# Attention scores of a fused attention and mixture-of-experts kernel: q and k handed over transposed, three 64-row products per head instead of two 128-row ones

## The chip, the cores and the metric

The kernel runs on one core of a Trainium2 chip. The engines that matter here are TensorE (PE, its weight loads are listed as PEld), VectorE (DVE), ScalarE (ACT), GpSimd (POOL), and SyncE (SP), which issues the DMA transfers. The metric is the time of one execution on the device in microseconds (us). The inputs are arranged on the host before the launch, and that is outside the measured time.

## What is computed

Attention with a block-causal mask, then a routed expert layer, then a dense layer with an x·sigmoid(x) activation. The change concerns the attention scores alone.

```python
def _attn_ref(q, k, v):                      # B, H, S, D = 4, 8, 576, 64
    scores = np.matmul(q, k.transpose(0, 1, 3, 2)) / np.sqrt(D)
    mask = pos[:, None] // 64 >= pos[None, :] // 64
    scores = np.where(mask, scores, -1e9)
    attn = softmax(scores)
    return np.matmul(attn, v)
# x = attention output, one row of 512 per token (2304 tokens)
# moe:  expert = argmax of a cosine score over 8 experts; out = gate * relu(x @ w1[e]) @ w2[e]
# moe2: h = x @ w_in; out = (h * sigmoid(h)) @ w_out
```

## The kernel before

**Stages.** The program first does the attention and then, in one long stage, the two layers behind it. The attention works on 16 pairs of heads (4 batches, 4 pairs each; the two heads of a pair are called hh = 0 and 1 here). A loop over i overlaps five steps of different pairs: the loads and splits of pair i + 3, the transposes of pair i + 2 (`x_units`), scores and softmax of pair i + 1 (`s_units`), the transposes of the probabilities of pair i (`v_units`), the products with v of pair i - 1 (`o_units`), and the scaling and expert scores of pair i - 2 (`e_units`). Beside these the loop converts one piece of a weight per pair (`conv`, tiles `wbits` and `wcv`).

**Precision.** A product of two fp32 numbers is made of fp32r products: each operand is split into a high part (`hi`, the fp32r rounding) and a low part (`lo`, the rest), and hi·hi, hi·lo and lo·hi are summed in PSUM.

**Scores before.** q and k of a pair arrive with tokens in the partitions and 64 numbers along the row. `split` writes hi and lo beside each other, [64 hi, 64 lo] for q and [64 lo, 64 hi] for k, so that a row is 128 wide. `x_units` transposes such 128×128 blocks on PE (9 for k, 9 for q of each pair) into PSUM, and ACT or DVE copies them to `QT` and `KT`: partitions 0 to 63 of q are hi, 64 to 127 are lo, and k the other way round. One product of 128 rows of `QT` and `KT` thus gives hi·lo + lo·hi. The second product uses `QH` and `KH`: hi parts in partitions 0 to 63, copied there by a DMA from `QT` and `KT` (`again`, tiles `qh` and `kh`), and the mask in partitions 64 to 127. So a head needs two products per score tile.

**Score units.** For a pair there are these units in `s_units`: `full(0)` and `full(1)` (128 queries, 576 keys, one head each, two pieces of 288 columns), `both(3)`, `both(2)`, `both(1)` (both heads, 448, 320 and 192 keys, the last computed as 256 columns) and `tiny` (64 keys). Each takes a PSUM tile `s` of two banks from the pool `ps_s`, which has two of them; head 0 lies in the first bank and head 1 in the second, and for `full` both banks hold one head. DVE takes the row maxima (`mx<-s`), ACT the exponentials with their sums (`p<-s,mx`), and then the PSUM tile is free.

**Order.** The class `_Plan` records all operations and sets their order on each engine from estimated costs (`_cost`); where an operation may run on ACT or DVE (`copy`, `either`), it chooses the engine by the estimated loads. Each engine then executes its instructions in that order. Nearly all instructions carry the line of the place where the plan issues them, L189, so they are told apart by their tiles.

**Names in the rows below.** `xk`, `xq`: transposes of k and q. `k0s`, `q0s`: splits of the first 64 tokens. `ks`, `qs`: splits. `pt`: transposes of probabilities. `o`: products with v. `e`: scaling and expert scores. `h`: the first product of the stage behind the attention. A form 128*64 means a product whose output takes 64 columns of the array, and 64*128 one that uses 64 of its rows.

Of the kernel before, what the change touches and what calls it, by code (L numbers as in the profile page):

```python
# [19 lines left out]
P = 128  # L20
# [59 lines left out]
class _Plan:  # L80
# [187 lines left out]
    def _cost(self, engine, method, args, kw):  # L268
# [20 lines left out]
        if engine == "tensor":  # L289
# [7 lines left out]
            if args[2].dtype == F32R:  # L297
                return max(n + 32, 2 * free(args[1])) / 2.4
# [190 lines left out]
def _attention(first, ctx, late, tc, plan, q, k, v, emb, tau, x_dram, identr, lr_all, ss_all, conv=None):  # L489
# [12 lines left out]
    sp = pool("a_split", 2, first)  # L502
# [8 lines left out]
    qk = pool("a_qk", 2, ctx)  # L511
    hi_p = pool("a_hi", 1, ctx)
# [10 lines left out]
    def load(i, what):  # L523


        b, hp = pairs[i]
        src = {"q": q, "k": k, "v": v}[what]
        t = (vp if what == "v" else ld).tile([P, 8, D], F32, tag=what, name=f"{what}_{i}")
        body = src[b, 2 * hp:2 * hp + 2, 64:S, :]
        rows = t.rearrange("p (h j) d -> p h j d", h=2)  # L530
# [9 lines left out]
    heads = {}  # L540

    def head(b, src, what):

        if what != "v":
            heads[b, what] = t = ld.tile([P, NPAIR, D], F32, tag=what + "0",
                                         name=f"{what}0_{b}", bufs=1)
        for hh in range(2):
            r0 = 64 * hh
            nc.sync.dma_start(
                (v0[b % 2][:, :, r0:r0 + 64] if what == "v" else t)[r0:r0 + 64],  # L550
                src[b, :, 0:64, :].rearrange("(a h) p d -> p h a d", h=2)[:, hh])
# [14 lines left out]


    QH, KH = ([hi_p.tile([P, 2, w], F32R, name=f"{n}{m}") for m in range(2)]
              for n, w in (("qh", S + 64), ("kh", S)))

    def masks(m, eq, ek):
# [1200 lines left out]
```

## Time and profile before

| | |
|---|---|
| median of 3 runs | 944.27 us (942.07 to 944.77) |
| profiled execution | 942.74 us, its span 941.0 us |
| PE busy over the span | 895.1 us (95%) |
| DVE busy | 747.8 us (79%) |
| ACT busy | 591.2 us (63%) |
| POOL busy | 107.0 us (11%) |
| share of 16 DMA engines, transfers issued by SP | 25.1% |

A busy time is the union of an engine's instructions. On PE the end of a matmul is modelled and includes the way through the array, so that neighbours overlap; what a matmul takes of PE's time is read from the distance between the starts of neighbours. The busy share of an engine is not the same in all stages, so the stages are read one by one.

### The profile page before, as it was taken

The page shows a single profiled execution, that of the slowest core. Times are in us where ns is not written, and L with a number is a line of the kernel's source. Part 1 is how long each engine was busy: PE and PEld are TensorE (multiplying, and loading weights), DVE is VectorE, ACT ScalarE, POOL GpSimd, SP SyncE. Part 2 cuts the span into 40 slices and gives each one's busy share as a digit, 9 for nine tenths or more (in the row PEclk, how much of TensorE's full clock was granted, in tenths as well). Part 3 has the DMA queues.
Part 4 walks back from the last instruction along what each step waited for, and adds up shares of the span by engine and source line. Part 5 has one row for each costly group of instructions (what it writes and reads, how often), then busy time and mean ns, then how long its engine had stood idle before and what let it go on. Part 6 is the DMA issues. An engine that isn't in the chain of part 4 may idle for free.

```text
span 941.0 us, 14120 instructions
## 1 busy us (share of the span) xinstructions
PE 895.1 (95%) x4890; PEld 744.3 (79%) x4890; DVE 747.8 (79%) x1367; ACT 591.2 (63%) x1214; POOL 107.0 (11%) x166
## 2 busy tenths in 40 slices
PE   2999999999889998999999999999999999999996
PEld 2777677776556787888888888888899998898895
DVE  6788989987798987999978888888666666667663
ACT  4878888887656765888876566676434334334332
POOL 4010111112200001010311111121101001001001
PEclk9999999999999999999999999999999999999998
DMA  6446657536224234775100033131211002000000
GB/s 179 121 127 165 176 137 215 134 117 230 75 86 145 101 112 154 266 250 172 54 27 23 23 111 133 41 125 62 78 46 51 18 1 64 4 1 34 1 0 34
DMA packets 67051, 91.63 MB, mean 97 GB/s; under 512 B 28888, under 2 KB 45272, under 8 KB 66976
## 3 DMA queue, kind: packets, MB, share of 16 engines
q1 hardware_dynamic: 61536, 72.32, 25.1%
q0 software_dynamic: 5440, 18.36, 5.6%
q8 instruction: 40, 0.66, 0.3%
q14 instruction: 35, 0.29, 0.1%
HBM read 123.23 MB, written 13.11 MB: 145 GB/s over the span
## 4 chain that ended last, share of the span: by engine, by line
PE 59%; issue 0%; DVE 0%; ACT 0%; POOL 0%; POOLq 0%; ACTq 0%
PE o L189 20%; PE g L189 19%; PE y L189 9%; PE h L189 9%; PE ht L189 1%; PE yt L189 1%; PE xt L189 1%; POOL out_dram L1524 0%; POOLq L1767 0%; DVE sg L189 0%; DVE ht L189 0%; ACT sg L189 0%; DVE yt L189 0%; DVE xt L189 0%; ACT ys L189 0%
## 5 line engine op out<-in xcount | busy, mean ns | idle before, releaser
L189 PE MATMUL o<-w,g 128*128 128x512 f32 x864 | 229.9, 398 | 0.0
L189 PE MATMUL g<-yt,w 128*128 128x384 f32 x1152 | 227.3, 337 | 0.2 <-issue 0.2
L189 PEld LDWEIGHTS g<-yt,w 128*128 128x128 f32 x1152 | 203.3, 188 | 13.0 <-issue 0.5
L189 PEld LDWEIGHTS o<-w,g 128*128 128x128 f32 x864 | 161.2, 189 | 31.0 <-DVE g L189 0.7
L189 ACT ACTIVATE sg<-g 128x384 f32<-128x384 f32 x96 | 47.4, 493 | 142.6 <-PE g L189 142.1
L189 PE MATMUL y<-w2s,ht 128*128 128x512 f32 x450 | 128.6, 400 | 0.7 <-DVE w2s L189 0.7
L189 PE MATMUL h<-w1s,xt 128*128 128x512 f32 x450 | 110.4, 396 | 0.7 <-ACT xt L189 0.5
L189 DVE TENSOR_TENSOR w1s<-wraw,w1s 128x1024 fp32r<-128x1024 f32 x75 | 91.5, 1223 | 19.3 <-ACT w1s L189 18.6
L189 PEld LDWEIGHTS h<-w1s,xt 128*128 128x128 f32 x450 | 84.2, 188 | 21.1 <-issue 1.7
L189 DVE TENSOR_TENSOR w2s<-wraw,w2s 128x1024 fp32r<-128x1024 f32 x75 | 91.2, 1223 | 11.6 <-ACT w2s L189 9.8
L189 PEld LDWEIGHTS y<-w2s,ht 128*128 128x128 f32 x450 | 81.1, 188 | 13.7 <-DVE w2s L189 1.0
L189 ACT ACTIVATE p<-s,mx 128x576 f32<-128x576 f32 (+4 forms) x160 | 83.1, 532 | 8.5 <-DVE mx L189 7.5
L189 DVE TENSOR_REDUCE mx<-s 128x1 f32<-128x576 f32 (+2 forms) x96 | 67.6, 709 | 20.8 <-PE s L189 16.4
L189 ACT CAST w2s<-wraw 128x1024 fp32r<-128x1024 f32 x66 | 69.4, 1053 | 19.7 <-PE h L189 8.5
L189 DVE TENSOR_TENSOR w<-win,w 128x512 fp32r<-128x512 f32 x96 | 65.9, 689 | 16.7 <-ACT w L189 16.6
L189 ACT CAST g<-sg 128x384 fp32r<-128x384 f32 x96 | 49.3, 514 | 43.9 <-DVE sg L189 43.0
L189 ACT CAST w1s<-wraw 128x1024 fp32r<-128x1024 f32 x61 | 64.4, 1059 | 17.8 <-PE y L189 7.8
L189 PE MATMUL o<-pt,v 128*64 128x256 f32 (+5 forms) x320 | 68.8, 450 | 0.2 <-ACT pt L189 0.2
L189 DVE TENSOR_TENSOR w<-wout,w 128x512 fp32r<-128x512 f32 x96 | 65.6, 683 | 2.5 <-ACT w L189 2.3
L189 ACT CAST w<-win 128x512 fp32r<-128x512 f32 x86 | 53.3, 622 | 21.3 <-PE o L189 21.0
L189 PE MATMUL pt<-ident,p 128*128 128x128 f32 (+1 forms) x400 | 61.6, 275 | 0.9 <-DVE pt L189 0.6
L189 DVE CAST w<-wout 128x512 fp32r<-128x512 f32 x53 | 22.6, 427 | 47.8 <-PE g L189 47.7
(208 smaller groups left out, 1293.1 us busy)
## 6 DMA issues: line engine op xcount, KB each, us to landing
wraw<-in_moe_w_dram SPq DMA_DIRECT2D x76, 1024.0 KB
wbits<-in_moe_w_in_dram SPq DMA_DIRECT2D x16, 512.0 KB
wbits<-in_moe_w_out_dram SPq DMA_DIRECT2D x16, 512.0 KB
kh<-kt SPq DMA_DIRECT2D x15, 288.0 KB
k<-in_k_dram SPq DMA_DIRECT2D x16, 256.0 KB
q<-in_q_dram SPq DMA_DIRECT2D x16, 256.0 KB
v<-in_v_dram SPq DMA_DIRECT2D x32, 128.0 KB
x_rows<-xe POOLq DMA_DIRECT2D x4, 1024.0 KB, 7.0
```

What stands on the lines that cost most here:

```text
L189: alts = {e: (lambda eng, m=m, a=a, k=k: getattr(eng, m)(*a, **k), self._cost(e, m, a, k), self._shares(e, m, a, k)) for e, m, a, k in calls}
```

## The change

The host passes q and k of each pair already transposed (`_layout`): partitions 0 to 63 hold the 64 numbers of head 0, partitions 64 to 127 those of head 1, and the 576 tokens lie along the row. The parts of v are rearranged on the host too, so that a partition's row is one piece of memory. `x_units`, `QT`, `KT`, `QH`, `KH`, their masks and the DMA copies `again` are gone. `split` makes hi and lo of a [128, 576] tile, as [128, 2, 576], with q scaled by 0.125 on the way. `scores` issues for each head three products of 64 rows (hi·hi, hi·lo, lo·hi), head 0 in PE's rows 0 to 63 and head 1 in rows 64 to 127, in turn, and a product of 64 columns from `maskq` and `maskk`, two constants, that adds the mask where a tile has one. All calls of a unit are recorded as one operation (`together`), and a 64-row fp32r product is estimated at half its cost. `full` now does both heads at once and takes both PSUM tiles of `ps_s`; `both(1)` computes 192 columns instead of 256. The loop starts at i = -2 instead of -3.

```diff
+    def together(self, calls):
+        costs = [self._cost("tensor", "matmul", c[:3], {}) for c in calls]
+        def f(eng):
+            for out, a, b, kw in calls:
+                eng.matmul(out, a, b, **kw)
+        self.call({"tensor": (f, sum(costs))}, [self._box(x) for c in calls for x in c[1:3]],
+                  list(dict.fromkeys(self._box(c[0]) for c in calls)))
...
             if args[2].dtype == F32R:
-                return max(n + 32, 2 * free(args[1])) / 2.4
+                part = 0.5 if args[1].shape[0] == 64 else 1.0
+                return max(n + 32, 2 * free(args[1])) / 2.4 * part
...
-    sp = pool("a_split", 2, first)
...
-    qk = pool("a_qk", 2, ctx)
-    hi_p = pool("a_hi", 1, ctx)
+    sp = pool("a_split", 3, ctx)
     ps_s = pool("ps_s", 2, ctx, space=PSUM)
...
         if what == "v":
-            for hh in range(2):
-                nc.sync.dma_start(rows[:, hh], body[hh].rearrange("(j p) d -> p j d", p=P))
+            t = vp.tile([P, 8, D], F32, tag=what, name=f"{what}_{i}")
+            nc.sync.dma_start(t, v[b, hp, :, 0:8, :])
...
         else:
-            nc.sync.dma_start(rows, body.rearrange("h (p j) d -> p h j d", p=P))
-        if hp == 0:
-            head(b, src, what)
+            t = ld.tile([P, S], F32, tag=what, name=f"{what}_{i}")
+            nc.sync.dma_start(t, {"q": q, "k": k}[what][b, hp])
...
-    def split(n, what, key, t, **kw):
-        hi, lo = (0, 1) if what == "q" else (1, 0)
-        spl[key] = s = sp.tile([P, n, 2, D], F32R, **kw)
-        nc.vector.tensor_copy(s[:, :, hi, :], t)
-        nc.sub(s[:, :, lo, :], t, s[:, :, hi, :].bitcast(F32))
+    def split(i):
+        t = raw[i, "k"]
+        spl[i, "k"] = s = sp.tile([P, 2, S], F32R, tag="k", name=f"ks_{i}")
+        nc.copy(s[:, 0], t)
+        nc.sub(s[:, 1], t, s[:, 0].bitcast(F32))
+        t = raw[i, "q"]
+        spl[i, "q"] = s = sp.tile([P, 2, S], F32R, tag="q", name=f"qs_{i}")
+        nc.either(("scalar", "activation", (s[:, 0], t, AF.Copy), dict(scale=0.125)),
+                  ("vector", "tensor_scalar_mul", (s[:, 0], t, 0.125), {}))
+        nc.vector.scalar_tensor_tensor(s[:, 1], t, 0.125, s[:, 0].bitcast(F32), ALU.mult,
+                                       ALU.subtract)
...
-                for j in range(4):
-                    nc.tensor.transpose(ps[:, j * P:(j + 1) * P], s[:, 4 * hh + j], identr)
...
-            for z, qs, ks, q0 in ((0, QT[i], KT[i], 0), (1, QH[i % 2], KH[i % 2], 64 * odd)):
-                c = slice(q0 + qcols(j), q0 + qcols(j) + n)
-                for out, hh, c0, w in parts:
-                    nc.tensor.matmul(out, qs[:, hh, c], ks[:, hh, c0:c0 + w],
-                                     start=(z == 0), stop=(z == 1))
+            qs, ks = spl[i, "q"], spl[i, "k"]
+            c = slice(qcols(j), qcols(j) + P)
+            calls = []
+            for z, (m, n) in enumerate(((0, 0), (0, 1), (1, 0))):
+                for out, hh, c0, w, mask in parts:
+                    r = slice(64 * hh, 64 * hh + 64)
+                    calls.append((out, qs[r, m, c], ks[r, n, c0:c0 + w],
+                                  dict(start=(z == 0), stop=(z == 2))))
+                if z == 1:
+                    for out, hh, c0, w, mask in parts:
+                        r = slice(64 * hh, 64 * hh + 64)
+                        if mask is not None:
+                            calls.append((out[:, mask:mask + 64], maskq[r], maskk[r],
+                                          dict(start=False, stop=False)))
+            nc.together(calls)
...
-        def full(hh):
-            def f():
-                if hh == 0:
-                    alloc()
-                ps = ps_s.tile([P, 2, 512], F32, tag="s", name=f"s4{hh}_{i}")
-                scores(4, *[(ps[:, a, 0:288], hh, 288 * a, 288) for a in range(2)])
+        def full():
+            alloc()
+            ps = [ps_s.tile([P, 2, 512], F32, tag="s", name=f"s4{hh}_{i}") for hh in range(2)]
+            scores(4, *[(ps[hh][:, a, 0:288], hh, 288 * a, 288, (64, 224)[hh] if a == hh else None)
+                        for a in range(2) for hh in range(2)])
+            for hh in range(2):
...
-        return [(0.55, full(0)), (0.55, full(1)), (0.8, both(3)), (0.6, both(2)),
+        return [(1.1, full), (0.8, both(3)), (0.6, both(2)),
                 (0.5, both(1)), (0.45, tiny)]
```

**PE in the middle of the attention.** Before, from the second score unit of pair 6 on (`s41_6`, `s3_6`, `s2_6` are its units; the numbers behind a unit's name are its pair and a buffer):

```order
L189 MATMUL s41_6_435<-kt_6_386,qt_6_385 128x288 x2
L189 MATMUL s41_6_435<-kh0_137,qh0_135 128x288 x2
L189 MATMUL xk1_7_437<-ident_62,ks_7_378 128x128 x4
L189 MATMUL o_4_432<-pt_4_380,v_4_333 64x512 x2
L189 MATMUL s3_6_440<-kt_6_386,qt_6_385 128x448 x2
L189 MATMUL s3_6_440<-kh0_137,qh0_135 128x448 x2
L189 MATMUL pt2_5_438<-ident_62,p_5_382 128x128 x4
L189 MATMUL xk2_7_442<-ident_62,k0s_1_274 128x128
L189 MATMUL o_4_432<-pt_4_380,v_4_333 64x384 x2
L189 MATMUL xq0_7_445<-ident_62,qs_7_379 128x128 x4
L189 MATMUL s2_6_446<-kt_6_386,qt_6_385 128x320 x2
L189 MATMUL s2_6_446<-kh0_137,qh0_135 128x320 x2
```

Now, from the last score units of pair 5 on:

```order
L189 MATMUL o_4_353<-pt_4_315,v_4_273 64x512 x2
L237 MATMUL s1_5_327<-ks_5_274,qs_5_275 128x192 x4
L237 MATMUL s1_5_327<-maskk_128,maskq_127 128x64 x2
L237 MATMUL s1_5_327<-ks_5_274,qs_5_275 128x192 x2
L237 MATMUL s0_5_333<-ks_5_274,qs_5_275 128x64 x6
L189 MATMUL pt0_5_347<-ident_62,p_5_310 128x128 x4
L189 MATMUL pt1_5_355<-ident_62,p_5_310 128x128 x4
L189 MATMUL o_4_353<-pt_4_315,v_4_273 64x384 x2
L189 MATMUL pt2_5_358<-ident_62,p_5_310 128x128 x4
L189 MATMUL pt4_5_365<-ident_62,p_5_310 128x128 x4
L237 MATMUL s40_6_349<-ks_6_308,qs_6_309 128x288
L237 MATMUL s41_6_350<-ks_6_308,qs_6_309 128x288
```

The transposes `xk` and `xq` are gone, two score units often stand next to each other, and in the units of two heads (here `s40_6` and `s41_6`) the heads take turns product by product.

**ACT at the same place.** Before, from pair 6's second copy of k on (`qt`, `kt` are the copies out of PSUM, `p` the exponentials):

```order
L189 CAST kt_6_386<-xk1_6_392 128x512
L189 ACTIVATE p_5_382,rs_139<-s40_5_383,mx_5_4_0_384 128x576
L189 COPY pt_4_380<-pt2_4_395 128x512
L189 ACTIVATE p_5_382,rs_139<-s41_5_393,mx_5_4_1_394 128x576
L189 COPY pt_4_380<-pt3_4_399 128x512
L189 ACTIVATE p_5_382,rs_139<-s3_5_397,mx_5_3_0_398 128x448 x2
L189 ACTIVATE qt_6_385<-xq0_6_400 128x512
L189 ACTIVATE p_5_382,rs_139<-s2_5_401,mx_5_2_0_402 128x320 x2
L189 ACTIVATE qt_6_385<-xq1_6_405 128x512
```

Now, for the same pair 5:

```order
L189 CAST ks_7_342<-k_7_305 128x576
L189 COPY pt_4_315<-pt4_4_329 128x512
L189 ACTIVATE qs_7_343<-q_7_306 128x576
L189 COPY pt_4_315<-pt3_4_326 128x512
L189 ACTIVATE p_5_310,rs_129<-s40_5_311,mx_5_4_0_313 128x576
L189 ACTIVATE p_5_310,rs_129<-s41_5_312,mx_5_4_1_314 128x576
L189 COPY ot_3_330<-o_3_317 128x512
L189 COPY pt_4_315<-pt6_4_335 128x64
L189 COPY ot_3_330<-o0_3_336 128x64
L189 ACTIVATE p_5_310,rs_129<-s3_5_321,mx_5_3_0_322 128x448 x2
L189 ACTIVATE p_5_310,rs_129<-s2_5_324,mx_5_2_0_325 128x320 x2
```

The copies `kt` and `qt` no longer stand between the exponentials; the first operation of a split (`ks`, `qs`) may now run on ACT, two pairs ahead of its use.

**ACT at the start.** Now, from the first split on (`wbits`, `wcv` belong to the weight conversion, `en_s` to the expert embedding):

```order
L189 ACTIVATE qs_139<-q_126 128x576
L189 ACT_TABLE_LOAD
L189 ACTIVATE en_s<-en_s 8x1
L189 CAST ks_146<-k_136 128x576
L189 ACT_TABLE_LOAD
L189 ACTIVATE en_s<-en_s 8x1
L189 ACTIVATE qs_147<-q_137 128x576
L189 CAST ks_165<-k_143 128x576
L189 ACTIVATE p_148,rs<-s_0_149,mx_4_0_151 128x576
L189 ACTIVATE p_148,rs<-s_0_150,mx_4_1_152 128x576
L189 ACTIVATE wcv_218<-wbits_217 128x512
L189 ACTIVATE wbits_217<-wbits_217 128x512
```

Before, `wcv` and `wbits` stood ahead of the first exponentials of pair 0; now a split of pair 2's k (`ks_165<-k_143`) stands there, and `wcv` behind the first two.

## Rows read from the trace of the kernel before

**Rows 1.** Stages: length, busy us (instructions) by engine, granted clock, DMA share, GB/s.

```profile
31.00:216.00 185.00, 180.63 (x1303) 139.51 (x1301) 165.14 (x401) 154.87 (x464) 19.81 (x18) 1.00 0.55 153
...
246.00:941.00 695.00, 671.16 (x3315) 572.36 (x3313) 544.14 (x860) 401.70 (x664) 69.81 (x85) 0.99 0.23 77
```

**Rows 2.** The page's chain of work that ended last: shares by engine.

```profile
PE 59%; issue 0%; DVE 0%; ACT 0%; POOL 0%; POOLq 0%; ACTq 0%
```

**Rows 3.** PE in time: start us, us, operation, form, count [idle before, releaser].

```profile
8.52 1.25 PE L189 MATMUL xk<-ident,ks 128*128 128x128 f32 x8 [8.52 <-DVE ks L189]
...
15.56 0.85 PE L189 MATMUL s<-kt,qt 128*128 128x288 f32 x2 [0.18 <-ACT qt L189]
...
23.79 1.12 PE L189 MATMUL s<-kt,qt 128*128 128x448 f32 x2 [4.78 <-ACT p L189]
...
31.30 0.53 PE L189 MATMUL s<-kt,qt 128*128 128x288 f32 x2 [0.15 <-ACT p L189]
...
216.04 0.53 PE L189 MATMUL s<-kt,qt 128*128 128x288 f32 x2 [0.69 <-ACT p L189]
...
245.75 3.60 PE L189 MATMUL h<-wraw,x 128*128 128x512 f32 x8
```

**Rows 4.** PE in time within one pair, from 104.8 to 114.6 us.

```profile
104.81 0.39 PE L189 MATMUL s<-kh,qh 128*128 128x64 f32 x2
105.03 1.09 PE L189 MATMUL pt<-ident,p 128*128 128x128 f32 x8
...
108.27 0.42 PE L189 MATMUL s<-kh,qh 128*128 128x288 f32 x2
108.62 0.27 PE L189 MATMUL pt<-ident,p 64*128 64x64 f32 x1
...
109.19 1.12 PE L189 MATMUL o<-pt,v 128*128 128x512 f32 x2
110.15 0.60 PE L189 MATMUL pt<-ident,p 128*128 128x128 f32 x4
110.51 0.54 PE L189 MATMUL xk<-ident,ks 128*128 128x128 f32 x4
110.89 0.50 PE L189 MATMUL s<-kt,qt 128*128 128x288 f32 x2
111.23 0.43 PE L189 MATMUL s<-kh,qh 128*128 128x288 f32 x2
111.50 0.60 PE L189 MATMUL pt<-ident,p 128*128 128x128 f32 x4
112.02 1.08 PE L189 MATMUL o<-pt,v 128*64 128x512 f32 x4
113.03 0.28 PE L189 MATMUL xk<-ident,k0s 128*128 128x128 f32 x1
113.15 0.63 PE L189 MATMUL s<-kt,qt 128*128 128x448 f32 x2
113.62 0.57 PE L189 MATMUL s<-kh,qh 128*128 128x448 f32 x2
114.03 0.60 PE L189 MATMUL pt<-ident,p 128*128 128x128 f32 x4
```

**Rows 5.** Attention by groups: operation, forms, count | busy us, mean ns | idle before.

```profile
L189 DVE TENSOR_TENSOR ks<-k,ks 128x512 fp32r<-128x512 f32 x16 | 12.7, 796 | 0.0
...
L189 ACT ACTIVATE qt<-xq 128x512 fp32r<-128x512 f32 x32 | 19.1, 602 | 4.5 <-PE xq L189 4.5
...
L189 ACT CAST kt<-xk 128x512 fp32r<-128x512 f32 x24 | 14.1, 588 | 3.3 <-PE xk L189 2.9
...
L189 ACT ACTIVATE wcv<-wbits 128x512 f32<-128x512 f32 x12 | 8.1, 677 | 4.4 <-DMA wbits<-in_moe_w_in_dram 4.4
```

**Rows 6.** The same groups for the softmax of one unit, `both(3)`.

```profile
L189 DVE TENSOR_REDUCE mx<-s 128x2 f32<-128x896 f32 x16 | 17.4, 1087 | 8.1 <-PE s L189 6.4 <-ACT qt L189 1.5 <-ACT wcv L189 0.2
...
L189 ACT ACTIVATE p<-s,mx 128x448 f32<-128x448 f32 x32 | 20.0, 633 | 1.0 <-DVE mx L189 0.8
```

More of the change, by code (lines that the diff above doesn't have):

```diff
@@ L538, in load @@
         raw[i, what] = t
[L540 to L551, printed above, removed]
-    spl = {}
@@ L583, in _attention @@
-    masks(0, nc.vector, nc.gpsimd)
-    plan.shift = 60
-    masks(1, nc.gpsimd, nc.gpsimd)
-    plan.shift = 0
+    maskq = cp.tile([P, P], F32R, name="maskq")
+    maskk = cp.tile([P, 64], F32R, name="maskk")
+    nc.vector.memset(maskq.bitcast(F32), 0.0)
+    nc.gpsimd.memset(maskk.bitcast(F32), 0.0)
+    for r0 in (0, 64):
+        nc.vector.memset(maskq.bitcast(F32)[r0:r0 + 1, 0:64], NEG)
+        nc.gpsimd.memset(maskk.bitcast(F32)[r0:r0 + 1], 1.0)
     rs = cp.tile([P, B, 5, H], F32, name="rs")
@@ L702, in _attention @@
+    PR, PT, OT, XE, LG = {}, {}, {}, {}, {}
     WID = {j: 2 * P * j + P for j in (4, 3, 2, 1)}
@@ L771, in tiny @@
             rows = slice(r0, r0 + 64)
-            out = slice(0, r0 + 64)
-            scores(0, (ps[out, 0, 0:64], 0, 512, 64), (ps[out, 1, 0:64], 1, 0, 64))
+            scores(0, (ps[:, 0, 0:64], 0, 512, 64, None), (ps[:, 1, 0:64], 1, 0, 64, None))
             c0 = PO[0]
@@ L944, in inter @@
         return _merge([(1.0, f) for _, f in a], [(1.0, f) for _, f in c])
-    for i in range(-3, NP + 2):
-        if i == -3:
+    for i in range(-2, NP + 2):
+        if i == -2:
             esq = experts()
@@ L950, in _attention @@
             expert_rows(esq)
-        if 0 < i + 4 < NP:
+        if 0 < i + 3 < NP:
             for w in "kq":
-                load(i + 4, w)
+                load(i + 3, w)
         if 0 <= i + 1 < NP:
             load(i + 1, "v")
-        if i + 3 < NP:
+        if i + 2 < NP:
             plan.shift = SPS if i > SPS_I else 0
-            for w in "kq":
-                split(8, w, (i + 3, w), raw[i + 3, w], tag=w, name=f"{w}s_{i + 3}")
+            split(i + 2)
             plan.shift = 0
-        if 0 <= i + 2 < NP and pairs[i + 2][1] == 0:
-            b = pairs[i + 2][0]
-            for w in "kq":
-                split(NPAIR, w, (b, w + "0"), heads[b, w], tag=w + "0", name=f"{w}0s_{b}", bufs=1)
-        xt = x_units(i + 2) if 0 <= i + 2 < NP else []
         vt = v_units(i) if 0 <= i < NP else []
@@ L969, in _attention @@
         et = e_units(i - 2) if 0 <= i - 2 < NP else []
-        run(inter(_units(xt, vt), _units(et, st, ot)))
+        run(inter(vt, _units(et, st, ot)))
         if conv is not None:
             conv(i, ps_t)
-    return (ld, sp), (qk, hi_p, ps_s)
+    return (ld,), (sp, ps_s)
 def _units(*lists):
@@ L1746, with _layout @@
 _OUTS = [((NTOK, DM), "float32")]
+def _layout(name, a):
+    import numpy as _np
+    if name == "v":
+        a = a.reshape(B, NPAIR, 2, S, D)
+        body = a[:, :, :, 64:].reshape(B, NPAIR, 2, 4, P, D).transpose(0, 1, 4, 2, 3, 5)
+        first = a[:, :, :, :64].reshape(B, NPAIR, P, 1, D)
+        return _np.concatenate([body.reshape(B, NPAIR, P, 8, D), first], 3)
+    if name in "qk":
+        a = a.reshape(B, NPAIR, 2, S, D)
+        if name == "q":
+            a = _np.stack([_np.roll(x, -64 * (b % 2), 2) for b, x in enumerate(a)])
+        else:
+            tiles = [a[:, :, 0, 64 + P * t:64 + P * t + P] for t in (3, 2, 1, 0)]
+            a = _np.stack([_np.concatenate(tiles + [a[:, :, 0, :64]], 2), a[:, :, 1]], 2)
+        return a.transpose(0, 1, 2, 4, 3).reshape(B, NPAIR, P, S)
+    return a
 def kernel(**inputs):
```

101 lines of the change are left out of this document (10 added, 91 removed).

## The prediction, made before the changed kernel was run

> **What bounds the kernel now.** I read the chain of waits first: PE holds all of it that is followed, and no other engine and no wait has a share [rows 2]. The table by stages says the same of the part behind the attention: PE is busy 671 of 695 us there [rows 1]. Nothing in that part is changed, so whatever moves its first product `h`, at 245.75 us [rows 3], should move the end by as much. The question is the attention, 0 to 246 us.
>
> PE in order of time divides it into three parts [rows 3]. The start: the first transposes wait until 8.52 us for DVE's split of k, the first scores stand at 15.56, and pair 1's scores at 31.30. The steady part: pair 15's scores begin at 216.04, so a pair takes (216.04 - 31.30) / 14 = 13.20 us. The tail: 216.04 to 245.75, the last pairs' probabilities and outputs. In the steady 185 us PE is busy 180.6 (98%), DVE 165.1 (89%), ACT 154.9 (84%), and the granted clock is 1.00, the 2.4 GHz level [rows 1]. PE is the bound, but DVE is close behind, so a cut on PE alone would be worth little; it counts only if DVE and ACT shrink too.
>
> **The change part by part.**
>
> *Transposes of q and k.* Four take 110.89 - 110.51 = 0.38 us, 0.095 each [rows 4]. A pair has 18, so PE loses 1.71 us per pair.
>
> *Scores as they are.* The four products of one head's 576 keys take 111.50 - 110.89 = 0.61 us, the four of 448 columns 114.03 - 113.15 = 0.88 [rows 4]. Between and beyond these I interpolate 0.66 for 320 and 0.56 for 256 columns; two products of 64 columns take 0.22 [rows 4], four 0.44. A pair: 2 × 0.61 + 0.88 + 0.66 + 0.56 + 0.44 = 3.76 us.
>
> *Scores as they will be.* A pair has 22 couples of 64-row products (one of each head): 6 of 288 columns, 3 each of 448, 320, 192 and 64, and 4 masks of 64. The trace has no couple in the row halves. Its two ends are one product's time and two products' time. Near the first end stands a row: two heads' products with v, each in half of the array's columns, take 113.03 - 112.02 = 1.01 us together, and one product over all columns, 110.15 - 109.19 = 0.96 [rows 4]. So halves of the columns work side by side, weight loads included; I take the same for halves of the rows, since the heads' outputs also lie in different PSUM banks. The second product of a score is 0.135 for 288 columns and 0.205 for 448 [rows 4], 0.15 for 320 in between. By that slope 64 columns would cost 0.04, but they take 0.11 [rows 4]; I read this as a floor, the pace of weight loads, and take 0.11 for 192 and 64. Sum: 6 × 0.135 + 3 × 0.205 + 3 × 0.15 + 10 × 0.11 = 2.98 us. To it come the exposed weight load of a block's first product, 0.34 / 2 - 0.27 / 2 = 0.035 for each of two [rows 4], 0.07 in some 3.5 blocks, 0.25; and the change between whole array and halves. Ahead of the one 64-row product of today, two products take 0.35 instead of 0.27 [rows 4], 0.08 for a change. The program's order has 137 such changes before and 194 now, 57 / 16 × 0.08 = 0.29 per pair. Together 3.5 us against 3.76 if couples run side by side, and 6.5 (2 × 2.98 + 0.54) if they don't.
>
> So PE loses 1.71 + 0.26 = 2.0 us per pair.
>
> The Trainium skill (TensorE: Matmul & The Clock Gate, Part 3: Packing small matmuls) gives 3.07 times for four row tiles. By that share a couple would take about 1.3 times one product, and 2.98 would be some 3.9; the column row above shows 1.05, and no row shows row halves.
>
> *Copies out of PSUM.* Per pair four of 512 columns go, 0.60 (`qt`, ACT) and 0.59 (`kt`) each [rows 5], and three short ones of at most half of that: 2.4 + 0.8 = 3.2 us of ACT and DVE. The splits remain, four operations of 576 instead of 512 columns: at 0.80 for the dearest [rows 5] that is at most 4 × 0.1 more, and the four small operations per batch on the first tokens, one per pair, pay for it. The first operation of a split may now be on ACT, at 0.68 × 576 / 512 = 0.76 [rows 5]. The plan can place copies on either engine, so I count 1.6 us less on each.
>
> *DMA.* The copies into `qh` and `kh` go, with their wait ahead of the second product; loads are fewer and longer. With a DMA share of 0.55 [rows 1] and loads issued a pair ahead, I count nothing. That cover is gone only at the start.
>
> *Steady part.* The three engines lose 2.0, 1.6 and 1.6 us of 13.2. The smallest cut decides where all are near full: 13.2 - 1.6 = 11.6 us per pair, 14 × 1.6 = 22.4 us. If PE's waits for copies of q and k go too, 2.1 (29 us); if the waits between score units grow, 1.0 (14 us).
>
> *Start.* k's split ends at about 8.5 [rows 3], and scores need only k's and q's splits: first scores at 8.5 instead of 15.56, 7 us. What follows in pair 0 stays bound by DMA: ACT now waits 4.4 us for `wbits` [rows 5], and PE 4.78 us for the exponentials behind it [rows 3]. In the new order ACT waits for pair 2's k, which stands behind the loads of pairs 0 and 1, and then for `wbits`. Its price lies between 3 us of the gain lost and 3 more won by the shorter list of loads; I take 7, bounds 4 and 10.
>
> *Tail.* No transposes of q or k are in it; 0.3 us, bounds -2 and +1.5.
>
> Sum: 942.74 - 22.4 - 7 - 0.3 = 913 us for the profiled execution. This lies 1.5 below the median of the three runs, so I say **914**; ends 942.7 - 29 - 10 - 1.5 = 902 and 942.7 - 14 - 4 + 2 = 927.
>
> **The rivals.**
>
> *The row halves do not overlap (slower).* Then scores cost 6.5 us, 2.7 more, against 1.7 saved: 1.0 us per pair, 15 pairs, +15, less 7 at the start: 951. It decides from a couple's price of 0.225 us (3.76 + 1.71 - 0.54, over 22) in the steady part, and 0.25 with the start counted in; 2 × 0.135 = 0.27 lies past it. For it: no row of row halves at work together. Against: the column row.
>
> *Only the weight loads queue up.* With 0.11 as the pace of weight loads, as above: if the two halves load in turn, no couple is below 0.22: 22 × 0.22 + 0.54 = 5.4, 1.6 more than now, just what the transposes give. Only the start remains: 936.
>
> *A half's next weights wait for its product.* Then each couple pays 0.11 on top: 22 × 0.11 = 2.4, scores 5.9, +0.45 per pair: 942.7 + 7 - 7 = 943, no change. Against it: in the rows of 288 columns a product every 0.135 leaves no room for a load in line [rows 4]. The Trainium skill says this (same page, same section: a weight load overlaps a running product only where the row group differs). By that rule the whole-array rows should be longer than they are, so the trace speaks against it here.
>
> *The ring of score tiles becomes the bound.* `full` now needs both PSUM tiles at once. A tile of 896 columns is held for 0.88 on PE [rows 4], 1.09 for the maximum and 2 × 0.63 for the exponentials [rows 6]: 3.2 us, 3.6 ns per column. The units in line in one buffer, 1152 + 896 + 384 columns, need 8.8 us without any wait, and a pair takes 11.6. It decides if the three units wait for ACT and DVE by more than 0.93 us each; at 1.3 us each a pair takes 12.7, the steady part gives 7 us, and the time is 929.
>
> **How the numbers follow.** Forecast 0.73; ring 0.08; queueing weight loads 0.06; weights behind their own half 0.03; no overlap 0.10. Faster by over 0.3% (2.8 us, about what a measurement of this kernel can tell from no change): 0.73 + 0.08 + 0.05 = 0.86; the same: 0.03; slower: 0.11. The forecast's own range is 902 to 927; with the ring and the queueing loads the range is 900 to 938, which leaves out no overlap, weights behind their half, and a little on the low side.
>
> **What would show it.** In the changed profile two 288-column products of `ks,qs` should start within some 0.01 us of each other and the next two 0.135 later; if all starts are 0.13 apart, there is no overlap. First scores near 8.5 us, pair 15's near 186, `h` near 216, with the later stage still 695 us long. ACT and DVE busy should be about 1.6 us less per pair. PE idle ahead of the first `s` of a pair, released by ACT's `p`, would show the ring. The prediction is wrong if the later stage, which starts with loads that follow from the routing, can't start 30 us earlier: the routing's small operations are spread over the last four pairs, and if they end later than the attention does, PE would stand idle ahead of `h`.

## The result, and the profile of the changed kernel

| | before | changed |
|---|---|---|
| median of 4 runs each | 943.17 us (941.86 to 944.77) | 920.98 us (919.93 to 923.15) |
| profiled execution, its span | 942.74 us, 941.0 us | 920.62 us, 918.9 us |
| PE, DVE, ACT busy | 895.1, 747.8, 591.2 us | 879.6, 726.5, 567.2 us |
| DMA packets | 67051 | 38250 |

The ratio is 0.9767 (0.9741 to 0.9793): the changed kernel is 22 us faster. PE in time, the answer to [rows 3]; the columns are start, us, operation, form, count, and in brackets the idle time ahead and what ended it:

```profile
5.70 1.33 PE L237 MATMUL s<-ks,qs 64*128 64x288 f32 x8 [5.70 <-ACT qs L189]
...
11.38 1.11 PE L237 MATMUL s<-ks,qs 64*128 64x448 f32 x4 [2.42 <-ACT p L189]
...
22.43 0.79 PE L237 MATMUL s<-ks,qs 64*128 64x288 f32 x8
...
189.39 0.53 PE L237 MATMUL s<-ks,qs 64*128 64x288 f32 x1 [0.29 <-ACT p L189]
...
222.53 1.88 PE L189 MATMUL h<-wraw,x 128*128 128x512 f32 x4
```

These are the same marks as before the change: first scores, pair 0's second unit, pair 1's scores, pair 15's scores, and `h`. Between them the account of the 22 us is complete:

| part | before | changed | difference | forecast |
|---|---|---|---|---|
| to pair 1's scores | 31.30 | 22.43 | -8.9 | -7 |
| to pair 15's scores (14 pairs) | 184.74, 13.20 each | 166.96, 11.93 each | -17.8 | -22.4 |
| to `h` | 29.71 | 33.14 | +3.4 | -0.3 |
| behind `h`, to the end of the span | 695.3 | 696.4 | +1.1 | 0 |

The same parts by stage, the answer to [rows 1]; the columns are length, busy us (instructions) of PE, weight loads, DVE, ACT and POOL, granted clock, DMA share, GB/s:

```profile
22.43:189.39 166.96, 162.49 (x1328) 113.23 (x1327) 149.17 (x326) 133.88 (x412) 20.95 (x18) 1.00 0.39 122
189.39:197.00 7.61, 7.42 (x30) 4.73 (x30) 3.89 (x15) 2.80 (x9) 0.00 (x0) 0.55 0.00 1
197.00:222.53 25.53, 24.09 (x181) 16.57 (x180) 15.74 (x55) 12.04 (x34) 7.01 (x8) 1.00 0.58 196
222.53:918.90 696.37, 672.61 (x3317) 572.59 (x3315) 543.50 (x858) 403.02 (x665) 69.98 (x85) 0.99 0.23 77
```

Three things are to be seen. PE still fills the steady part (162.5 of 167.0 us). DVE went from 165.1 of 185 us [rows 1] to 149.2 of 167, which is 11.8 to 10.7 us per pair, ACT from 11.1 to 9.6. And ahead of `h` there is a stretch of 7 us at about half the granted clock, which the kernel before does not have.

One pair's first score unit shows the two heads together. From the changed kernel, PE in time:

```profile
104.73 0.60 PE L189 MATMUL pt<-ident,p 128*128 128x128 f32 x4
105.26 0.80 PE L237 MATMUL s<-ks,qs 64*128 64x288 f32 x8
105.90 0.20 PE L237 MATMUL s<-maskk,maskq 64*128 64x64 f32 x2
105.93 0.50 PE L237 MATMUL s<-ks,qs 64*128 64x288 f32 x4
106.36 0.87 PE L189 MATMUL o<-pt,v 128*64 128x384 f32 x4
```

Eight products of 288 columns take 105.90 - 105.26 = 0.64 us, 0.16 for a couple. In the starts of the single records the two of a couple lie 0.003 to 0.004 us apart; the second couple follows 0.24 behind the first of the block, and each further one 0.13 behind the one before.

The waits of the steady part looked like a new bound at first. Total us, times, longest:

```profile
PEld pt L189 <- ACT p L189: 13.3, 20, 1.2
...
PEld s L237 <- ACT p L189: 10.3, 19, 1.6
```

PE's weight loads wait 23.6 us for exponentials; before, the loads of scores waited 4.3 us for them and those of the probabilities' transposes not at all. This is what the prediction named as the sign of the ring. But a weight load that waits does not stop a product that is running. The same table for the products themselves, in which a product counts as running to its modelled end, has only these:

```profile
PE s L237 <- ACT p L189: 2.3, 4, 1.5
PE pt L189 <- ACT p L189: 2.0, 6, 0.6
```

From start to start more is seen. Behind a transpose of probabilities of the whole array the next one mostly starts 0.109 us later, or 0.203 where the next product has another array shape. Starts that come more than 0.02 us later than that add up to 0.49 us per pair of lateness here, and to 0.07 in the kernel before.

So there were two theories for the steady part. A: the chain of scores, maxima, exponentials and the release of score tiles holds it. B: PE's own work holds it, and the waits are room that its queue already covers.

### The profile page after: what moved, and what is told of

The parts are those of the page before. It is cut to its first block, busy times and chain, and to the rows that moved or that the text cites. A ratio compares the mean times of both kernels' runs of the same rounds, so it can differ in the third digit from the quotient of the medians.

```text
span 918.9 us, 13841 instructions
## 1 busy us (share of the span) xinstructions
PE 879.6 (96%) x4922; PEld 717.7 (78%) x4922; DVE 726.5 (79%) x1289; ACT 567.2 (62%) x1155; POOL 103.1 (11%) x146
## 2 busy tenths in 40 slices
DMA packets 38250, 82.77 MB, mean 90 GB/s; under 512 B 5016, under 2 KB 13208, under 8 KB 38176
## 5 line engine op out<-in xcount | busy, mean ns | idle before, releaser
L189 DVE TENSOR_REDUCE mx<-s 128x1 f32<-128x576 f32 (+2 forms) x96 | 65.1, 707 | 16.0 <-PE s L237 11.5
L237 PE MATMUL s<-ks,qs 64*128 64x288 f32 (+4 forms) x576 | 65.3, 346 | 10.7 <-ACT qs L189 5.7
L189 PE MATMUL pt<-ident,p 128*128 128x128 f32 (+1 forms) x400 | 65.3, 291 | 3.8 <-ACT p L189 3.7
L237 PEld LDWEIGHTS s<-ks,qs 64*128 64x128 f32 x576 | 46.4, 196 | 26.6 <-ACT p L189 13.7
```

What stands on the lines that cost most here:

```text
L189: alts = {e: (lambda eng, m=m, a=a, k=k: getattr(eng, m)(*a, **k), self._cost(e, m, a, k), self._shares(e, m, a, k)) for e, m, a, k in calls}
L237: eng.matmul(out, a, b, **kw)
```

## Experiments

The steady part of every kernel, read like the table above (start of pair 1's and of pair 15's scores, over 14):

| kernel | median us | ratio to before | pair 1 | pair 15 | us per pair |
|---|---|---|---|---|---|
| before | 943.17 | 1 | 31.30 | 216.04 | 13.20 |
| changed | 920.98 | 0.9767 (0.9741 to 0.9793) | 22.43 | 189.39 | 11.93 |
| e1, heads not in turn | 928.73 | 0.9837 (0.9820 to 0.9853) | 22.82 | 197.35 | 12.47 |
| e5, one row half | 964.57 | 1.0241 (1.0188 to 1.0294) | 26.39 | 232.87 | 14.75 |
| e2, PE work back | 936.22 | 0.9919 (0.9902 to 0.9936) | 22.04 | 210.27 | 13.45 |
| e3, ACT work back | 922.49 | 0.9763 (0.9738 to 0.9788) | 24.83 | 191.79 | 11.93 |
| e4, DVE work back | 924.57 | 0.9788 (0.9771 to 0.9804) | 24.24 | 193.32 | 12.08 |
| e6, scores in the old form | 915.28 | 0.9718 (0.9679 to 0.9757) | 21.28 | 186.17 | 11.78 |
| e8, filler ahead of the tail | 917.20 | 0.9720 (0.9684 to 0.9756) | 23.09 | 191.00 | 11.99 |
| e9, v's layout alone | 947.52 | 1.0053 (1.0037 to 1.0070) | 34.94 | 221.15 | 13.30 |
| e7, fewer score blocks | 918.45 | 0.9752 (0.9714 to 0.9789) | 20.25 | 183.93 | 11.69 |
| e10, e7 and filler | 916.80 | 0.9732 (0.9703 to 0.9762) | 20.04 | 188.74 | 12.05 |
| e11, e10 and one block of products with v | 916.72 | 0.9723 (0.9699 to 0.9747) | 20.76 | 185.34 | 11.76 |
| e12, e11 in more rounds | 918.71 | 0.9743 (0.9716 to 0.9769) | 20.22 | 185.77 | 11.83 |

e11 and e12 are one kernel, and its pair differs by 0.07 us between two profiled executions: differences below 0.1 us per pair are not read, and those of 0.15 stand little above that.

### e1: the heads one behind the other

```diff
-            nc.together(calls)
+            nc.together([x for hh in range(2) for x, h in zip(calls, heads) if h == hh])
```

> The changed kernel with one difference: in each score unit all products of head 0 (PE rows 0 to 63) come before those of head 1 (rows 64 to 127), not in turn. Same products, same operands, same plan of all other work. Theory (the gain on PE comes from the two heads' products at work together in the row halves): the couples fall apart except where the last product of head 0 meets the first of head 1; scores go from 3.55 us per pair to between 5.5 and 6.5, so 1.9 to 2.9 us per pair more on an engine that is 97.5% busy, 16 pairs: 30 to 45 us, 950 to 965 us, slower than the kernel before. Rival (the halves don't matter, the scores are cheap because three 64-row products of one head cost little by themselves): within 3 us of 921.

928.73 us, 8 more than the changed kernel, 0.54 us per pair: neither theory. The trace says why. In the program a unit now has the first head's product hi·hi, hi·lo, its mask and lo·hi, and then the same four of the second head. PE in time, the unit of 448 and then the one of 576 keys:

```profile
62.04 0.69 PE L237 MATMUL s<-ks,qs 64*128 64x448 f32 x4
62.55 0.21 PE L237 MATMUL s<-maskk,maskq 64*128 64x64 f32 x2
62.58 0.85 PE L237 MATMUL s<-ks,qs 64*128 64x448 f32 x6
...
69.82 0.91 PE L237 MATMUL s<-ks,qs 64*128 64x288 f32 x5
70.45 0.19 PE L237 MATMUL s<-maskk,maskq 64*128 64x64 f32 x1
70.48 0.64 PE L237 MATMUL s<-ks,qs 64*128 64x288 f32 x5
70.96 0.19 PE L237 MATMUL s<-maskk,maskq 64*128 64x64 f32 x1
70.99 0.51 PE L237 MATMUL s<-ks,qs 64*128 64x288 f32 x2
71.43 0.33 PE L189 MATMUL pt<-ident,p 128*128 128x128 f32 x1
```

In the first three rows four products of 448 columns precede both masks, which is the order of the changed kernel, not that of this program: the second head's first product started 0.013 us after the first head's, ahead of three instructions that stand before it. In the unit of 576 keys, where each head has seven, the first three of head 0 ran alone and the second head joined at the fourth. This unit takes 71.43 - 69.82 = 1.61 us; the one of the changed kernel shown above takes 106.36 - 105.26 = 1.10, and the difference is nearly the whole 0.54 us per pair. So PE starts products of the two row halves past each other, over some four of them, and this run took only a part of the overlap away.

### e5: both heads in one row half

```diff
-                    r = slice(64 * hh, 64 * hh + 64)
+                    r = slice(0, 64)
```

> The changed kernel with one difference: head 1's products too read PE rows 0 to 63, so both heads of a pair get head 0's scores; number, size and order of all instructions stay. So no two products can lie in different row halves. After the run in which the order alone was changed (6 to 9 us more), two readings are open. Reading A (PE lets products of the two halves pass each other over a few places in its queue, so that run took only part of the overlap away): here all overlap goes, each of 22 couples costs 0.135 us more on average, 3.0 us per pair on an engine that is the bound: 14 to 15 us per pair instead of 11.93, 960 to 970 us in all. Reading B (64-row products are cheap one by one, the halves give only some 0.5 us per pair): 928 to 932.

964.57 us and 14.75 us per pair: reading A, at its number. The block that answers to the one shown of the changed kernel:

```profile
99.64 1.32 PE L237 MATMUL s<-ks,qs 64*128 64x288 f32 x8
100.81 0.30 PE L237 MATMUL s<-maskk,maskq 64*128 64x64 f32 x2
100.95 0.77 PE L237 MATMUL s<-ks,qs 64*128 64x288 f32 x4
101.65 0.66 PE L189 MATMUL pt<-ident,p 128*128 128x128 f32 x4
```

The eight products take 1.17 us instead of 0.64. Without the overlap the change would have made the kernel 2.4% slower than before. The pair is 2.82 us longer; the granted clock stood at half for some 5.5 us of this steady part (60.1 to 63.5 us, and from 230.8 on), which makes at most 0.2 of it.

### e2, e3, e4: work put back on one engine at a time

```diff
+        xt = x_units(i + 2) if 0 <= i + 2 < NP else []
-        run(inter(vt, _units(et, st, ot)))
+        run(inter(_units(xt, vt), _units(et, st, ot)))
```

where `x_units` holds, per pair, 18 transposes on PE (e2), two operations of 512 columns on ACT (e3) or two on DVE (e4).

> The changed kernel with PE work put back: the 18 transposes of 128x128 per pair that the change removed, of the new split tiles into the PSUM tiles of the ring that the probabilities' transposes use; nobody reads them, no copies, no DMA. It adds 18 x 0.095 = 1.7 us of PE per pair, 16 pairs: 27 us. Theory A (the steady part is now held by the chain from scores over maximum and exponentials to the release of the score tile, and PE's 1.2 us per pair of waits would take up part of the work): +8 to +16 us, 929 to 937. Theory B (PE alone is the bound, what looks like waits would only move): +24 to +30, 945 to 951.

> The changed kernel with ACT work put back: two activations of 512 columns per pair (0.68 us each, 1.36 per pair, 22 us over 16 pairs), from a split tile into a tile that nobody reads. No PE, no DVE, no DMA work. Theory A (the exponentials stand on the chain that holds the steady part): most of it shows, +12 to +22 us, 933 to 943, though ACT is busy only 80% there. Theory B (PE alone is the bound, ACT has 20% to spare): +0 to +4, 921 to 925.

> The changed kernel with DVE work put back: two subtractions of 512 columns per pair (0.68 us each by rows of like size, 1.4 per pair, 22 us over 16 pairs), from a split tile into a tile that nobody reads. No PE, no ACT, no DMA work. Theory A (the maxima stand on the chain that holds the steady part, and DVE is busy 89%): +10 to +22 us, 931 to 943. Theory B (PE alone is the bound): DVE would have 1.3 us per pair to spare, so +0 to +5, 921 to 926.

e2: 13.45 us per pair, 1.52 more, of 1.57 that 18 transposes take at the 0.087 us between their starts. e3: nothing, and e4 0.15, though the added operations ran (0.63 to 0.77 us each). The planner answered e3 and e4 by moving other copies between ACT and DVE; ACT and DVE together still did 0.5 and 0.8 us more per pair. For ACT the growth was 0.64 in e3 and 0.56 in e4; for DVE it was 0.24 in e4 alone, so e4 says little of DVE by itself. That work found room. PE's found little: e2 also has 14.1 changes of PE's array shape per pair instead of 11.9, at 0.094 us each (shown under e6), so it adds some 1.57 + 0.21 = 1.78 us, of which 1.52 show. The rest fits the waits: the lateness of the transposes of probabilities fell from 0.49 to 0.18 us per pair. The steady part goes by theory B in the main. The weight loads' waits are mostly no loss, but about 0.3 us per pair of them was time that PE could use.

As a total, e2 lies in theory A's range (936.22 of 929 to 937) and not in B's: 15 us more, though its steady part is 14 × 1.52 = 21 us longer. The total misleads here. 2.7 us came back in its tail, which from 210.27 to `h` at 240.64 is 30.4 us long instead of 33.1, with the granted clock at 1.00, and 2.5 us behind `h`, where 4.2 us less stand at the half clock. The tail is e8's question.

### e6: the scores in the old form, without the transposes

```diff
-            for z, (m, n) in enumerate(((0, 0), (0, 1), (1, 0))):
...
+            for z in range(2):
+                for out, hh, c0, w, mask in parts:
+                    calls.append((out, qs[:, z, c], ks[:, z, c0:c0 + w],
+                                  dict(start=(z == 0), stop=(z == 1))))
```

> The changed kernel with scores in the old form: for each head two products over all 128 rows (hi with hi, lo with lo, both heads' rows summed) in place of three of 64 rows, and no mask products; the scores differ from the reference, sizes and number of maxima, exponentials and all else stay. Changes of PE's array shape fall from 194 to 122. Theory (the new form of the scores costs PE more than the old one, because every unit now pays two changes of array shape of 0.09 us and more exposed weight loads; the gain of the change is the transposes alone): 0.3 to 0.5 us per pair less, 11.4 to 11.6, 913 to 917 us. Rival (the forecast's reckoning, new form 0.25 us per pair cheaper than the old one): 12.1 to 12.2 per pair, 923 to 926 us.

915.28 us, inside the theory's range, and 11.78 us per pair, 0.15 less than the changed kernel, where the theory had 0.3 to 0.5 and the forecast's reckoning 0.25 more. So the sign is the theory's and the size is half. It splits the change's steady gain: everything but the three-product form (the transposes, the copies, and `both(1)` with 192 columns for 256) is worth 13.20 - 11.78 = 1.42 us per pair, and the form gives 0.15 of that back. e2 is a second measure of the form: with all 18 transposes back its pair takes 13.45 us, 0.25 more than the kernel before.

The total is less clear. The intervals of e6 and of the changed kernel overlap, and of the 7.6 us between the profiled executions the steady part is only 2.1: the start gives 1.1 more and the tail 5.4, and the later stage takes 1.0 back. In the tail e6 kept the granted clock at 1.00; e8, below, gets 2.7 of those 5.4 us by that alone.

Where PE's time goes is seen if each product is given the time from its start to the start of the next one. Over the steady part, in us per pair:

| | before | e6 | changed | e5 |
|---|---|---|---|---|
| score products | 4.03 | 3.83 | 3.55 | 6.51 |
| transposes of probabilities | 2.85 | 3.26 | 3.58 | 3.40 |
| products with v | 3.26 | 3.45 | 3.57 | 3.60 |
| scaling and expert scores | 1.06 | 1.18 | 1.22 | 1.24 |
| transposes of q and k | 1.98 | 0 | 0 | 0 |

The score products themselves are 0.28 cheaper in the new form than in e6; the work beside them takes 0.48 longer, and 1.20 longer than in the kernel before.

What the new form pays is seen at its edges. In the changed kernel, four transposes with a product of the whole array behind them, and four with a 64-row product behind them:

```profile
41.78 0.66 PE L189 MATMUL pt<-ident,p 128*128 128x128 f32 x4
42.36 0.52 PE L237 MATMUL s<-ks,qs 64*128 64x64 f32 x6
...
45.38 0.66 PE L189 MATMUL pt<-ident,p 128*128 128x128 f32 x4
45.87 0.90 PE L189 MATMUL e<-rmat,ot 128*128 128x144 f32 x6
```

0.58 against 0.49 us: 0.09 for the change of the array's shape, and the same again on the way out. Over all starts of the steady part a transpose is followed after 0.109 us (median) by another and after 0.203 by a 64-row product, which makes 0.094. The records hold 8.0 such changes per pair before, 11.9 after and 7.3 in e6. The lateness of the transposes of probabilities is 0.34 us per pair in e6, against 0.49 and 0.07.

### e8: filler ahead of the tail

```diff
+        xt = x_units(i + 2) if i in (12, 13) else []
-        run(inter(vt, _units(et, st, ot)))
+        run(inter(_units(xt, vt), _units(et, st, ot)))
```

> The changed kernel with 36 transposes of 128x128 that nobody reads, put among PE's work in two iterations only, those ahead of the scores of the last two pairs (i = 12 and 13), 0.087 us each, 3.1 us of PE work in all. Theory (the granted clock falls to half from 189.5 to 196.3 us since PE idled just before, waiting for exponentials; with filler it doesn't): granted clock 1.00 through the tail, from pair 15's scores to h 30 to 30.5 us instead of 33.1; the filler costs 1 to 3 us in the steady part; 918 to 921 us in all. Rival (the clock falls for another reason): clock still about 0.57 there, tail 33 us, 922 to 924 us.

917.20 us; the tail takes 30.4 us (191.00 to 221.40), as the theory has it. First the tail of the changed kernel, PE in time, from the last small score units of pair 14 on:

```profile
186.97 0.47 PE L237 MATMUL s<-ks,qs 64*128 64x192 f32 x4 [1.51 <-ACT p L189]
...
187.99 0.52 PE L237 MATMUL s<-ks,qs 64*128 64x64 f32 x6 [0.33 <-ACT p L189]
...
190.10 1.33 PE L237 MATMUL s<-ks,qs 64*128 64x288 f32 x7 [0.19 <-ACT p L189]
...
193.16 1.92 PE L189 MATMUL o<-pt,v 128*128 128x512 f32 x2
```

The last row is the same work as the row of 1.12 us in [rows 4]. Then the ten us ahead of pair 15's scores, changed kernel first, and e8, with e8's first 7.5 us behind them:

```profile
179.39:189.39 10.00, 7.87 (x74) 5.44 (x70) 8.75 (x24) 8.93 (x30) 1.84 (x2) 1.00 0.43 144
```

```profile
181.00:191.00 10.00, 9.97 (x83) 6.78 (x82) 8.30 (x21) 8.47 (x27) 2.40 (x3) 1.00 0.42 144
...
191.00:198.50 7.50, 7.18 (x51) 4.65 (x52) 7.36 (x34) 3.50 (x11) 0.00 (x0) 1.00 0.01 3
```

And the same ten us of e6, without transposes and without filler, with its tail behind them; then those of e4, with the stretch from 194.70 us on:

```profile
176.17:186.17 10.00, 8.26 (x59) 6.73 (x59) 7.67 (x21) 9.39 (x33) 0.00 (x0) 1.00 0.31 100
...
186.17:213.87 27.70, 27.25 (x184) 18.55 (x183) 17.95 (x63) 13.82 (x37) 6.29 (x8) 1.00 0.48 171
```

```profile
183.32:193.32 10.00, 8.52 (x72) 5.56 (x71) 8.84 (x19) 8.85 (x27) 2.60 (x3) 1.00 0.43 147
194.70:201.50 6.80, 6.49 (x34) 5.07 (x33) 5.25 (x14) 2.81 (x9) 0.00 (x0) 0.50 0.00 0
```

PE was busy 7.87 of 10 us, and the clock then stood at 0.55 for 7.6 us; with filler it was busy 9.97, and the clock stayed at 1.00, the 2.4 GHz level. e2, with its transposes in the same place, shows the same. So do the single runs: the mean granted clock of an execution is 0.990 to 0.994 in the four of e8, and 0.985 or 0.986 in the four of the changed kernel. In the kernel before, PE was busy 9.3 of the ten us and the clock held, with the transposes of q and k among PE's work there. So filler in this place keeps the clock up. That PE's busy share in these ten us decides is not shown: e6 held the clock after 8.26 in its profiled execution, and e4 lost it after 8.52. Nor does e6 seem to hold it each time: its four runs have mean clocks of 0.992, 0.990, 0.985 and 0.984, and the last two take 2.5 to 5.4 us longer than the first two.

### e9: v's layout alone

```diff
-            for hh in range(2):
-                nc.sync.dma_start(rows[:, hh], body[hh].rearrange("(j p) d -> p j d", p=P))
+            nc.sync.dma_start(t, v[b, hp, :, 0:8, :])
```

> The kernel before with one part of the change alone: v rearranged by the host so that a partition's row is one piece of memory, one load per pair instead of two. q, k, the transposes and the scores stay. Theory (the DMA queues have room in the steady part, PE sets the pace): within 2 us of before, 941 to 945. Rival (v's many short packets hold up the loads at the start): the first scores or pair 1's scores move up, 2 to 5 us less, 938 to 941.

947.52 us, 5 more than the kernel before: neither expectation. Pair 1's scores come 3.6 us later (34.94), which is most of it; the steady part is 0.1 per pair longer. ACT in time:

```profile
13.81 0.26 ACT L189 ACTIVATE qh<-xq 64x128 fp32r<-64x128 f32 x1
19.90 0.66 ACT L189 ACTIVATE wcv<-wbits 128x512 f32<-128x512 f32 x1 [5.83 <-DMA wbits<-in_moe_w_in_dram]
20.46 0.64 ACT L189 ACTIVATE wbits<-wbits 128x512 int32<-128x512 uint32 x1
21.00 0.58 ACT L189 ACTIVATE qt<-xq 128x512 fp32r<-128x512 f32 x1
```

The planner put the weight conversion ahead of two copies of `qt`, which in the kernel before stand at 14.91 and 15.88, and its load is not there before 19.9: the first scores wait until 21.64. So the part of the change that concerns v brings nothing by itself. What it does beside the new q and k, where the order at the start is another, no run separates.

### e7, e10, e11, e12: fewer blocks on PE

e7 lets the units of 448 and 64 keys share a score tile, and those of 320 and 192; e10 adds e8's filler; e11 and e12 give all products with v of a pair to PE in one block.

```diff
-        return [(1.1, full), (0.8, both(3)), (0.6, both(2)),
-                (0.5, both(1)), (0.45, tiny)]
+        return [(1.1, full), (1.25, pair(3, 0)), (1.1, pair(2, 1))]
...
-        return [(0.9, begin), (0.9, key(1)), (0.7, key(2)),
-                (0.7, lambda: (key(3)(), key(4)())), (0.2, tiny)]
+        return [(3.2, body), (0.2, tiny)]
```

> The changed kernel with fewer score blocks: the units of 448 and 64 keys share one score tile and stand together on PE, those of 320 and 192 too; products, maxima and exponentials stay. Changes of array shape fall from 194 to 175, and a pair takes 4 score tiles from the ring instead of 6. Theory (PE's time is the bound, and its shape changes with it): 19 x 0.094 = 1.8 us and some exposed weight loads less, 916 to 919 us. Rival (the ring of score tiles is the bound): a tile is held longer, by the maximum and exponentials of a second unit, but taken less often; between 4 us less and 8 us more, 917 to 929 us, with PE idle ahead of scores.

> The kernel with fewer score blocks and, in the two iterations ahead of the last two pairs' scores, the 36 filler transposes that nobody reads. Theory (the two gains, 2.5 and 3.8 us alone, are different places, shape changes and the clock of the tail): 914 to 917 us, granted clock 1.00 from pair 15's scores to h. Rival (with fewer blocks PE idles less there and the clock holds without filler, which then only costs 3 us): 918 to 922.

> As the kernel with fewer score blocks and filler, and with the products with v of a pair in one block on PE, not in four; changes of array shape fall from 178 to 117. Theory (PE is the bound of the steady part and a change costs it 0.094 us): 61 x 0.094 = 5.7 us less than the kernel without this, 908 to 912. Rival (a block of 1.8 us in one piece keeps scores and probabilities waiting, and the maxima and exponentials behind them come late): no gain or a loss, 914 to 922.

> The kernel with fewer score blocks, filler and one block of products with v once more, in more rounds, to tell whether it beats the changed kernel, whose ratio to the kernel before is 0.9767 (0.9741 to 0.9793). If its gain of some 4 us is real: ratio 0.970 to 0.974. If it is the scatter of few runs: 0.975 to 0.979.

e7 gave 11.69 us per pair, 0.23 less, where 19 changes of shape over 16 pairs are 0.11, and 2.5 us in the median. Its 918.45 lies in the ranges of both theories, so it does not decide between them. e10 held its range of 914 to 917. e11 gave 0.1 us instead of 5.7. Its steady part is 0.29 us per pair shorter than e10's, and e12's 0.22, of 0.36 that 61 changes over 16 pairs make. But the attention's last product starts at 216.8 us instead of 219.4, so there less than half of the gain was left, and of that the later stage took back most. In e7 and its successors `h` moves up to 209 to 212 us, ahead of the last scaling products, but the routing does not follow:

```profile
229.96 0.75 PE L189 MATMUL tok<-r_tok_rhs,r_rows 128*128 128x38 bf16 x18 [4.16 <-DVE r_tok_rhs L189]
```

That is e7, where PE waits 4.16 us for DVE's routing operations; the changed kernel waits 2.31 us in that place. Over six runs the last version (e12) came to 0.9743 (0.9716 to 0.9769), between its two expectations. That interval overlaps the changed kernel's, and so does e8's (0.9684 to 0.9756). None of these versions beats the changed kernel for certain. By the medians the filler alone is worth 3.8 us.

## Why the prediction was right, and where its steps were off

The time (920.98 against 914) lies in the range and the sign is right. The gain is 22 us where 29 were forecast. Three steps failed: what lies beside the scores, the rule of the smallest cut, and the tail.

- **Couples side by side: right.** 0.16 us per couple of 288 columns with the block's edge, 0.13 from couple to couple, and without overlap (e5) the score products take 6.51 us per pair, where the prediction's rival had 6.5; the pair grew by 2.82. What that rival describes is thus what e5 shows, at 965 us; its 951 had the pair 1.0 us longer than before, where e5's is 1.55 longer. The rival with weight loads in turn (0.22 per couple) falls by the same row. So does the one with weights behind their own half: in e5 all products lie in one half, and they follow each other after 0.146 us, which is hardly more than the 0.13 of the couples. The Trainium skill (TensorE: Matmul & The Clock Gate, Part 3: Packing small matmuls) says that a weight load overlaps a running product only in another row group; e5's row speaks against it. An estimate from the 3.07 times that the same section of the Trainium skill gives for four tiles was that a couple takes 1.3 times one product; here it is 0.64 / 4 against 1.17 / 8, 1.1 times.
- **Scores in the new form: right in themselves, wrong beside them.** The score products take 3.55 us per pair (forecast 3.5), and 0.28 less than in e6's old form (forecast 0.26). Yet e6's pair is 0.15 shorter. The step that failed is that all other work of PE was left as it was: beside the scores it takes 1.20 us per pair longer than before, which with 1.98 for the transposes and 0.48 for the scores leaves 1.26, the 1.27 that were found. Two causes are seen. The changes of shape were counted at 57 / 16 × 0.08 = 0.29 and are 3.9 × 0.094 = 0.37. And the lateness of the transposes of probabilities behind the exponentials grew from 0.07 to 0.49, which the sum had at nothing and the prediction named only as a bound ("if the waits between score units grow"). The rest is not traced and stays open.
- **Transposes: 1.71 forecast.** They held 1.98 us of PE's time per pair before, from start to start; 18 neighbours at the 0.087 between their starts are 1.57, and the 0.095 of [rows 4] holds the first one's load. What the pair gained by losing them is less, 1.42 (e6) to 1.52 (e2), since other work took longer.
- **"The smallest cut decides": wrong step, near number.** ACT lost 1.5 us per pair and DVE 1.1, against 1.6 forecast for each, and PE 1.3. By the rule DVE's cut would be the bound. e3 shows that ACT was not: its work grew by 0.64 us per pair and the pair did not grow. For DVE the evidence is e2, where PE's work made the pair longer and DVE's did not stand in the way; e4 added only 0.24 to DVE and cost 0.15. PE's own cut decides. That the 1.6 of the wrong rule stood nearer to it than the 2.0 that the forecast had for PE is luck. A busy share of 89% looked like a second bound, and was not seen to act as one.
- **Start: 7 forecast, 8.9 found,** inside its bounds. The first scores stand at 5.70, not 8.5. Before, k's load had landed at 3.51 us by its semaphore, but DVE filled `qh` with the mask's rows until 5.47 and split k only then; those fills are gone. DVE in time, before and then changed:

```profile
4.46 1.01 DVE L189 MEMSET qh<- 64x512 f32 x4 [0.16 <-DVE rs L189]
5.51 1.22 DVE L189 CAST ks<-k 128x512 fp32r<-128x512 f32 x1
```

```profile
3.60 0.49 DVE L189 CAST ks<-k 128x576 fp32r<-128x576 f32 x1 [1.42 <-DMA k<-in_k_dram]
```

- **Tail: outside its bounds** (-2 to +1.5, found +3.4). The prediction said only that no transpose of q or k is in it. It did not count on the granted clock: with no transposes ahead of the tail PE was busy 7.87 of ten us, the clock then went to half, and filler in that place (e8) gives 2.7 us back. Why e6's profiled execution kept its clock without filler stays open.
- **The ring: not the bound.** The sign that I had named for it (waits for `p`) came, as 23.6 us of waits on the weight loads, 4.3 on the products and the late starts above. But PE's work put back lengthened the pair by most of its price (e2), and ACT's, which would hold the tiles longer, did not (e3). e7 does not settle it.
- **Later stage: 1.1 us longer.** It started 23 us earlier and kept its length, as forecast.

## What to carry to other kernels

When an engine looks full, put back a known amount of its work, and of its neighbours' in turn: here 1.52 of some 1.78 us per pair came back on PE, and 0 and 0.15 of the 0.5 and 0.8 on ACT and DVE together, which no busy share and no table of waits had told. Read such a test by the stage and not by the total, and look at what the planner did with the rest. Products of 64 rows in both halves of PE cost hardly more than one, but each block of them between whole-array work pays two changes of shape of 0.09 us, so count blocks as well as products. Beside the products that a change removes, look at how far apart those that stay now start. Work that is removed may have been what kept PE's clock up; look at the granted clock of the stretch behind.

## What the runs showed of the hardware

- Products in different row halves start out of program order, over some four products (e1: the fifth instruction of a unit started 0.013 us after the first). The Trainium skill (TensorE: Matmul & The Clock Gate, Part 3: Packing small matmuls) says that products start and end in program order; in e1 they don't start in it. The ends of products are modelled, so no row tells in which order they end.
- A change of PE's array shape costs 0.094 us at full clock. The Trainium skill (TensorEngine Tiling (Array Packing), Tiling Modes) says that such a change drains the engine; the rows, in which the extra is the same behind a transpose (0.109 and 0.203) and behind 512 columns (0.430 and 0.523), agree and add the price.
- After ten us with PE busy 7.87 of them, and single waits of at most 1.51 us, the granted clock went to half for 6.8 us, and the same work took 1.92 instead of 1.12 us. With filler (9.97 of ten) it stayed at 1.00, the 2.4 GHz level. In the profiled execution of e6 it stayed there after 8.26 of ten too.
